# Grouped-query decode attention: K transposed on VectorE in 32x32 blocks of 4-byte words, scores and PV with K and V as the moving operand

## The chip, the cores and the metric

The kernel runs on one core of one Trainium2 chip. The metric is the device time of one execution in microseconds, as the median of a few executions. The profile's span (first to last instruction of the program) is about 1.8 us shorter than that time.

## The reference, cut to what matters

Two tokens (batch 2, one query each) attend to a long cache: 32 query heads share 8 K/V heads (`rep` = 4), 32,768 keys per head, head size 128, all bf16. A small MLP makes a gate.

```python
q = (x @ wq).reshape(B, Sq, Hq, Dh).transpose(0, 2, 1, 3)
scores = einsum("bhqd,bhkd->bhqk", q, repeat(k_cache, 4)) * Dh ** -0.5
o = einsum("bhqk,bhkd->bhqd", softmax(scores), repeat(v_cache, 4))
s = o.transpose(0, 2, 1, 3).reshape(B, 1, Hq * Dh) @ wo
...                                   # g = silu(MLP(layernorm(x)))
return x + s * g
```

K and V are 134 MB each, and every byte is used once. The weights are another 12 MB.

## The kernel before

The cache is cut into 32 pairs of a 4 MB K tile and a 4 MB V tile (16,384 keys each). One tile is 32 KB in each of the 128 partitions: 128 keys of 128 values. Tiles rotate through five slots, all loaded by the SyncE queue. `wo` is the last load, in three parts, into a slot that a K tile gives up.

```python
t = slot(name)                                     # 5 slots of [128, 16384] bf16
nc.sync.dma_start(out=t, in_=cache[b, g, i*NK:(i+1)*NK, :].rearrange("(p t) d -> p (t d)", p=128))
...
for n in range(NQ):                                # small loads of x, on ScalarE's queue
    nc.scalar.dma_start(out=x4_bf[32*n:32*n+B, :], in_=A_x[:, 0, n*QW:(n+1)*QW])
...
def emit_k(n):                                     # one K tile: 16 blocks of 8 x 128 keys
    for blk in range(NBLK):
        for j in range(TPB):                       # TensorE transposes K ...
            nc.tensor.transpose(out=tT[:, j, :], in_=kt[:, blk*TPB + j, :], identity=ident)
        # ... VectorE (3 of 4) or ScalarE (1 of 4) copies it out of PSUM ...
        nc.vector.tensor_copy(out=ktb, in_=tT)
        for j in range(TPB):                       # ... and K is the stationary operand
            nc.tensor.matmul(sc[:, u*rep:(u+1)*rep], lhsT=ktb[:, j, :], rhs=q4)
    nc.scalar.activation(out=ep, in_=sc, func=ACT.Exp, scale=inv_sqrt_dh)
...
def emit_v(n, ep):                                 # one V tile, V stationary
    for u in range(KPT):                           # 128 matmuls of 4 columns
        nc.tensor.matmul(o, lhsT=vt[:, u, :], rhs=ep[:, u*rep:(u+1)*rep], ...)
```

The softmax here doesn't subtract the row's maximum and nothing guards it: scores larger than these inputs give would overflow.

## Time and profile before

| | before |
|---|---|
| time, median of 3 runs | 682.95 us (682.73 to 683.0) |
| span of the profiled run | 681.2 us |
| busy: PE / DVE / ACT | 80% / 43% / 23% |
| DMA rate in the middle | 428 GB/s |

The first lines are from the page: the span, the busy time of each engine, the DMA engines' mean busy share and rate in 40 equal slices, two of the DMA queues (packets, MB, share of the 16 engines' time), and the chain of waits that ended last.

```profile
span 681.2 us, 26832 instructions
PE 548.0 (80%) x12728; PEld 533.1 (78%) x12728; DVE 294.5 (43%) x476; ACT 154.7 (23%) x168; POOL 1.1 (0%) x9
...
DMA  7999999999999999999999999999999999999965
GB/s 308 430 428 427 429 428 427 430 424 429 431 424 428 427 434 428 426 428 429 428 428 425 432 430 427 428 427 425 428 427 428 424 426 429 430 428 429 420 256 182
...
q1 hardware_dynamic: 13804, 280.50, 96.8%
q8 instruction: 99, 1.62, 1.0%
...
DMA 57%; PE 35%; issue 5%; ACT 2%; DVE 0%; ACTq 0%; POOL 0%; SPq 0%; DVEq 0%; POOLq 0%
```

From the second slice to the 38th the DMA engines are full: 280.5 MB at 428 GB/s are 655 of the 681 us. PE is busy, but it is not what the kernel waits for.

The view by stretches shows the start and the end closer. Its columns are the stretch and its length, busy time (and instructions) of PE, PEld, DVE, ACT and POOL, the granted TensorE clock, the mean busy share of the 16 DMA engines, and GB/s.

```profile
12.00:14.00 2.00, 0.04 (x1) 0.04 (x2) 1.92 (x6) 0.00 (x0) 0.00 (x0) 1.00 0.00 0
...
648.00:652.00 4.00, 4.00 (x82) 4.00 (x81) 2.51 (x4) 1.05 (x2) 0.00 (x0) 0.77 0.91 341
652.00:656.00 4.00, 4.00 (x102) 3.92 (x99) 2.84 (x5) 1.99 (x2) 0.00 (x0) 1.00 0.55 225
656.00:660.00 4.00, 3.11 (x94) 2.88 (x92) 1.90 (x3) 1.61 (x2) 0.00 (x0) 1.00 0.56 235
660.00:664.00 4.00, 2.79 (x89) 2.70 (x88) 0.35 (x2) 0.00 (x0) 0.00 (x0) 0.51 0.44 183
```

DMA moves nothing from 12 to 14 us: the queue of loads has been waiting for the load of `wq` to land, 11.8 us in all (total, times, longest):

```profile
SPq L75 <- DMA wq<-in_A_wq_dram: 11.8, 1, 11.8
```

From 652 us on it is half idle, although the last V tile and `wo` are still to come. The timeline of the end says when they came (start, duration, engine, line; in brackets the idle time before and what ended it):

```profile
665.92 3.57 PE L261 MATMUL o<-ep,v 128*128 128x4 bf16 x128 [3.13 <-DMA v<-in_A_v_cache_dram]
...
671.53 2.25 PE L305 MATMUL s_ps<-wo,oT_sb 128*2 128x128 bf16 x64 [2.04 <-DMA wo<-in_A_wo_dram]
...
675.77 1.97 PE L305 MATMUL s_ps<-wo,oT_sb 128*2 128x128 bf16 x64 [1.99 <-DMA wo<-in_A_wo_dram]
```

The last V tile (V31, requested at 623.1 us) landed at 665.9 us, parts of `wo` at 671.5 and 675.7.

### The profile page before, as it was taken

The page shows a single profiled execution, that of the slowest core. Times are in us where ns is not written, and L with a number is a line of the kernel's source. Part 1 is how long each engine was busy: PE and PEld are TensorE (multiplying, and loading weights), DVE is VectorE, ACT ScalarE, POOL GpSimd, SP SyncE. Part 2 cuts the span into 40 slices and gives each one's busy share as a digit, 9 for nine tenths or more (in the row PEclk, how much of TensorE's full clock was granted, in tenths as well). Part 3 has the DMA queues.
Part 4 walks back from the last instruction along what each step waited for, and adds up shares of the span by engine and source line. Part 5 has one row for each costly group of instructions (what it writes and reads, how often), then busy time and mean ns, then how long its engine had stood idle before and what let it go on. Part 6 is the DMA issues. An engine that isn't in the chain of part 4 may idle for free.

```text
span 681.2 us, 26832 instructions
## 1 busy us (share of the span) xinstructions
PE 548.0 (80%) x12728; PEld 533.1 (78%) x12728; DVE 294.5 (43%) x476; ACT 154.7 (23%) x168; POOL 1.1 (0%) x9
## 2 busy tenths in 40 slices
PE   0598798878879888878988878888887898887884
PEld 0587788878878888878887878888787888887783
DVE  2272454434455444435544344554344454443440
ACT  0042321212222121222211222221222222222220
POOL 0000000000000000000000000000000000000000
PEclk9995887667888766778876678987667887776785
DMA  7999999999999999999999999999999999999965
GB/s 308 430 428 427 429 428 427 430 424 429 431 424 428 427 434 428 426 428 429 428 428 425 432 430 427 428 427 425 428 427 428 424 426 429 430 428 429 420 256 182
DMA packets 13954, 282.22 MB, mean 414 GB/s; under 512 B 1162, under 2 KB 5268, under 8 KB 5268
## 3 DMA queue, kind: packets, MB, share of 16 engines
q1 hardware_dynamic: 13804, 280.50, 96.8%
q8 instruction: 99, 1.62, 1.0%
q14 instruction: 11, 0.09, 0.0%
q10 hardware_dynamic: 40, 0.01, 0.0%
HBM read 280.50 MB, written 0.00 MB: 412 GB/s over the span
## 4 chain that ended last, share of the span: by engine, by line
DMA 57%; PE 35%; issue 5%; ACT 2%; DVE 0%; ACTq 0%; POOL 0%; SPq 0%; DVEq 0%; POOLq 0%
DMA k<-in_A_k_cache_dram 48%; PE tT L230 21%; PE o L261 7%; PE sc L222 6%; DMA wo<-in_A_wo_dram 6%; ACT ktb L233 2%; DMA x_bf<-in_A_x_dram 1%; DMA xn_120<-xn 1%; PE S L270 0%; PE s_ps L305 0%; ACTq L87 0%; DVE stats_ln_127 L116 0%; DVE xn L123 0%; ACTq L134 0%; SPq L293 0%
## 5 line engine op out<-in xcount | busy, mean ns | idle before, releaser
L230 PE MATMUL tT<-ident,k 128*128 128x128 bf16 x3840 | 340.4, 245 | 29.5 <-DMA k<-in_A_k_cache_dram 23.6
L235 DVE COPY ktb<-tT 128x1024 bf16<-128x1024 bf16 x384 | 260.0, 692 | 167.6 <-PE tT L230 167.4
L230 PEld LDWEIGHTS <-k 128*128 128x128 bf16 x3840 | 269.7, 111 | 32.8 <-DMA k<-in_A_k_cache_dram 25.5
L233 ACT COPY ktb<-tT 128x1024 bf16<-128x1024 bf16 x128 | 129.5, 1012 | 474.2 <-PE tT L230 474.2
L222 PE MATMUL sc<-q_sb,ktb 128*128 128x4 bf16 x4096 | 180.6, 166 | 27.0 <-ACT ktb L233 21.2
L222 PEld LDWEIGHTS <-ktb 128*128 128x128 bf16 x4096 | 159.9, 99 | 35.2 <-ACT ktb L233 23.9
L261 PE MATMUL o<-ep,v 128*128 128x4 bf16 x3968 | 113.2, 166 | 42.4 <-issue 39.3
L261 PEld LDWEIGHTS <-v 128*128 128x128 bf16 x3968 | 108.7, 102 | 45.1 <-issue 41.9
L255 DVE TENSOR_REDUCE s<-ep 128x4 f32<-128x512 bf16 x32 | 22.0, 686 | 69.1 <-ACT ep L243 69.1
L275 DVE RECIPROCAL rec<-S 128x4 f32<-128x4 f32 x16 | 2.9, 183 | 59.9 <-PE S L270 59.9
L276 DVE TENSOR_TENSOR oT_sb<-o,rec 128x4 bf16<-128x4 f32 x16 | 2.6, 165 | 58.4 <-PE o L261 58.4
L243 ACT ACTIVATE ep<-sc 128x512 bf16<-128x512 f32 x32 | 19.1, 597 | 15.9 <-PE sc L222 15.9
L270 PE MATMUL S<-s,ones_f 128*128 128x4 f32 x64 | 18.0, 354 | 0.5 <-DVE t_f L204 0.5
L230 PE MATMUL tT<-ident,k_92 128*128 128x128 bf16 x128 | 11.5, 248 | 7.1 <-DMA k_92<-in_A_k_cache_dram 7.1
L270 PEld LDWEIGHTS S<-s,ones_f 128*128 128x128 f32 x64 | 16.0, 312 | 0.7 <-DVE t_f L204 0.7
L230 PEld LDWEIGHTS <-k_92 128*128 128x128 bf16 x128 | 9.1, 112 | 7.2 <-DMA k_92<-in_A_k_cache_dram 7.2
L146 PE MATMUL treg<-ident,xn_bf 2*128 2x2 bf16 x4 | 0.3, 171 | 14.0 <-DVE xn_bf L138 14.0
L146 PEld LDWEIGHTS <-xn_bf 2*128 2x128 bf16 x4 | 0.2, 113 | 14.0 <-DVE xn_bf L138 14.0
L230 PE MATMUL tT<-ident,k_94 128*128 128x128 bf16 x128 | 9.6, 218 | 0.8 <-issue 0.8
L305 PE MATMUL s_ps<-wo,oT_sb 128*2 128x128 bf16 x128 | 4.1, 306 | 4.1 <-DMA wo<-in_A_wo_dram 4.0
L230 PEld LDWEIGHTS <-k_94 128*128 128x128 bf16 x128 | 7.3, 97 | 0.0
L305 PEld LDWEIGHTS <-oT_sb 128*2 128x2 bf16 x128 | 3.1, 116 | 4.9 <-issue 2.7
(54 smaller groups left out, 40.6 us busy)
## 6 DMA issues: line engine op xcount, KB each, us to landing
v<-in_A_v_cache_dram SPq DMA_DIRECT2D x31, 4096.0 KB, 37.3
k<-in_A_k_cache_dram SPq DMA_DIRECT2D x30, 4096.0 KB
wq<-in_A_wq_dram SPq DMA_DIRECT2D x1, 4096.0 KB, 12.2
k_92<-in_A_k_cache_dram SPq DMA_DIRECT2D x1, 4096.0 KB, 13.5
k_94<-in_A_k_cache_dram SPq DMA_DIRECT2D x1, 4096.0 KB
v_99<-in_A_v_cache_dram SPq DMA_DIRECT2D x1, 4096.0 KB
w_96<-in_B_w_dram SPq DMA_DIRECT2D x2, 1792.0 KB
wo<-in_A_wo_dram SPq DMA_DIRECT2D x1, 2048.0 KB
```

Of the source, the lines that this page charges most:

```text
L146: nc.tensor.transpose(out=treg[:, c:c + B], in_=src[0:B, k::DK], identity=ident[0:B, 0:B])
L222: nc.tensor.matmul(sc[:, u * rep:(u + 1) * rep], lhsT=ktb[:, j, :], rhs=q4, start=True, stop=True,)
L230: nc.tensor.transpose(out=tT[:, j, :], in_=kt[:, blk * TPB + j, :], identity=ident[:, :])
L233: nc.scalar.copy(out=ktb[:, :, :], in_=tT[:, :, :])
L235: nc.vector.tensor_copy(out=ktb[:, :, :], in_=tT[:, :, :])
L243: nc.scalar.activation(out=ep[:, :], in_=sc[:, :], func=ACT.Exp, scale=inv_sqrt_dh)
L255: nc.vector.tensor_reduce(out=state["s"][:, i, :], in_=ep[:, :].rearrange("p (t h) -> p h t", h=rep), axis=AX.X, op=ALU.add,)
L261: nc.tensor.matmul(o[:, :], lhsT=vt[:, u, :], rhs=ep[:, u * rep:(u + 1) * rep], start=(i == 0 and u == 0), stop=(i == NPART - 1 and u == K ...
L270: nc.tensor.matmul(S[:, :], lhsT=ones_f[:, :], rhs=state["s"][:, j, :], start=(j == 0), stop=(j == NPART - 1),)
L275: nc.vector.reciprocal(out=rec[:, :], in_=S[:, :])
L276: nc.vector.tensor_mul(out=oT_sb[:, g * rep:(g + 1) * rep, b], in0=o[:, :], in1=rec[:, :],)
L305: nc.tensor.matmul(s_ps[32 * n:32 * n + B, :], lhsT=oT_sb[:, h, :], rhs=wo3[:, h, n * QW:(n + 1) * QW], start=(h == 0), stop=(h == Hq - 1) ...
```

## The change

The intent is to take work from TensorE. VectorE transposes K in 32x32 blocks of 4-byte words (two bf16 values at a time). A stationary operand `z` of 128 columns holds the queries block by block, zeros elsewhere, and K streams past it 512 columns at a time: 32 matmuls per tile instead of 128 transposes and 128 score matmuls. For PV, 16 columns of probabilities (4 keys x 4 heads) are stationary, four such tiles stand beside each other in the array, and V streams 512 columns at a time: 32 matmuls instead of 128. The eight small loads of x and its normalized copy also move from ScalarE's to GpSimd's queue.

```diff
-        nc.scalar.dma_start(out=x4_bf[32 * n:32 * n + B, :], in_=...)
+        nc.gpsimd.dma_start(out=x4_bf[32 * n:32 * n + B, :], in_=...)
 ... (the same for xn4)
-            for j in range(TPB):
-                nc.tensor.transpose(out=tT[:, j, :], in_=kt[:, blk * TPB + j, :], identity=ident[:, :])
-            nc.vector.tensor_copy(out=ktb[:, :, :], in_=tT[:, :, :])      # or nc.scalar.copy
-            ...  nc.tensor.matmul(sc[:, u * rep:(u + 1) * rep], lhsT=ktb[:, j, :], rhs=q4, ...)
+        for r in range(NR):                                   # 8 per tile
+            T = ktp.tile([128, W], I32, tag="T", name="T")    # W = 1024 words
+            nc.vector.transpose(out=T..., in_=kt[:, r * W:(r + 1) * W]...)
+            for nb in range(NB):
+                for e in range(2):
+                    nc.tensor.matmul(sc[:, :], lhsT=z[:, nb, e, zc:zc + 128], rhs=Tb[:, nb, :, e], ...)
-        nc.scalar.activation(out=ep[:, :], in_=sc[:, :], func=ACT.Exp, scale=inv_sqrt_dh)
+        nc.scalar.activation(..., accum_out=rs[:, :])
+        nc.vector.transpose(out=pt..., in_=ep...)             # probabilities, 512 elements
 ...
-        for u in range(KPT):
-            nc.tensor.matmul(o[:, :], lhsT=vt[:, u, :], rhs=ep[:, u * rep:(u + 1) * rep], ...)
+        for u in range(KPT // VT):
+            nc.tensor.matmul(
+                o[32 * j:32 * j + VT * rep, :],
+                lhsT=pt[:, r, a * VT * rep:(a + 1) * VT * rep],
+                rhs=vt[:, u * VT:(u + 1) * VT, :].rearrange("p t d -> p (t d)"),
+                tile_position=(0, 32 * j), ...)
 ... (per head group: a copy of o out of PSUM and 4 matmuls that sum and transpose it)
```

## The prediction

> **What bounds the kernel now.** The loads. In the table of 40 slices the DMA row is full from the second slice to about the 37th, at 424 to 434 GB/s, while PE is busy 80% of the span, DVE 43%, ACT 23%. K and V are 268 MB, weights 12 MB: 280.5 MB at 428 GB/s is 655 of the 681 us. One K+V pair (8.4 MB) needs 19.6 us; PE works about 17 us of each 20 (the table by stretches). The chain of waits is 57% DMA, "k" and at last "wo". So what PE saves in the middle is worth nothing; only the first 20 and last 35 us can change.
>
> **What the change does per pair** (estimates).
> - Removes 128 PE transposes, 128 score and 128 PV matmuls (about 17 us of PE) and their PSUM copies.
> - DVE: 8 transposes of 1024 words. The trace's 512-element reduction takes 686 ns, about one element per cycle plus 0.15 us; the Trainium skill (VectorE: DVE Perf Modes, "The three transpose paths") gives 311 ns for a 128x128 bf16 transpose, which fits; no run has yet shown it for 4-byte words. So about 1.2 us each, 9.8 us, plus 0.7 us for the probabilities: with waits about 13 us.
> - PE: 32 matmuls of 512 columns for scores and 32 column-tiled ones for PV. The skill (TensorE: Matmul & The Clock Gate, Part 1) gives 216 ns each warm, 427 cold: scores 7 to 14 us, PV 2 to 6 us. I expect 9 to 14.
>
> Both stay below 19.6 us, so steady state stays DMA-bound at 428 GB/s. K's slot is freed by DVE instead of PE, about as soon. From issue to landing a load takes 37 us: four loads outstanding on five slots, much slack.
>
> **Start.** The trace shows DMA moving nothing from 12 to 14.2 us: the queue waits ("wq" 11.8 us, "xn" 7.3 us) before issuing K0, K1, V0. By program order, the changed kernel issues wq, K0, K1, w3, w4, V0 without waits, because the eight small x loads moved to the GpSimd queue. The first 20 us moved 6.4 MB at 320 GB/s; 18 us at 428 would be 7.7 MB: about 3 us gained. Risk: the small loads land late behind 20 MB and delay q.
>
> **Tail.** V31 lands at 665.9 us, with DMA engines only half busy from 652 on; wo lands at 675.8. wo waits for K30's slot, as before. After V31: column-tiled PV (about 4 us cold), a PSUM copy and four fp32 matmuls (about 3 us more than now), close to wo's landing. So the tail gives back 0 to 2 us.
>
> **Prediction:** about 680 us, range 672 to 690. Faster by over 2%: 5%; within 2%: 81%; slower: 14%.
>
> **What would show it.** DMA row full and about 428 GB/s in the middle; the hole at 12 to 14 us gone; DVE transposes about 1.2 us each, DVE near 50 to 60%; score matmuls 0.22 to 0.43 us apart; PE below 65%; ACT near 5%; the chain of waits still mostly DMA k and wo.
>
> **What would make it wrong.** A 4-byte transpose at two cycles per element (2.3 us, over 18 us per pair) makes DVE the limit: about 700 us. Score matmuls slowed by the 4-byte step of the moving operand, or PV tiles not overlapping, on a cold clock: PE near 20 us per pair. A late q starving the queue near 48 us: some 5 us. Faster by 2% would need the half-idle DMA tail to disappear.

## More of the kernel before

Every `matmul` and `transpose` is two TensorE instructions, a weight load and a matmul, so a pair of tiles costs 768 of them. The compiled program has 25,369 TensorE instructions in all.

## The result, and the profile after

| | before | after |
|---|---|---|
| time, median of 4 runs | 682.89 us (682.73 to 683.0) | 666.06 us (665.98 to 666.11) |
| span | 681.2 us | 664.2 us |
| PE / DVE / ACT busy | 80% / 43% / 23% | 61% / 51% / 8% |

The ratio is 0.9754, with a 95% interval of 0.9737 to 0.977: faster by 2.5%. (A ratio is the mean time of one kernel's fast runs over that of the other's of the same rounds, so not quite the ratio of the medians.)

The same lines of the page of the changed kernel, then three of its groups of instructions (count, busy us, mean ns of one):

```profile
span 664.2 us, 6171 instructions
PE 403.1 (61%) x2588; PEld 172.5 (26%) x2620; DVE 340.1 (51%) x403; ACT 50.1 (8%) x152; POOL 7.4 (1%) x19
...
DMA  9999999999999999999999999999999999999996
GB/s 377 413 438 436 423 433 434 426 433 434 426 434 428 430 435 430 427 434 433 428 433 428 432 433 428 431 434 427 432 433 425 433 432 429 432 430 431 434 403 199
...
q1 hardware_dynamic: 13804, 280.50, 98.8%
q8 instruction: 20, 0.33, 0.2%
...
DMA 73%; PE 16%; DVE 7%; issue 3%; ACT 0%; POOL 0%; SPq 0%; DVEq 0%; ACTq 0%; POOLq 0%
...
L280 DVE STREAM_TRANSPOSE T<-k 128x1024 int32<-128x1024 int32 x240 | 273.9, 1207 | 173.7 <-DMA k<-in_A_k_cache_dram 173.7
L288 PE MATMUL sc<-T,z_123 128*128 128x512 bf16 x496 | 149.7, 463 | 97.0 <-DVE T L280 93.5
...
L320 PE MATMUL o<-v,pt 128*16 128x512 bf16 x992 | 67.0, 418 | 4.8 <-DMA v<-in_A_v_cache_dram 4.8
```

The stretches of the start and the end, and the end's timeline:

```profile
12.00:14.00 2.00, 0.00 (x0) 0.00 (x0) 0.00 (x0) 0.00 (x0) 0.00 (x0) 1.00 1.04 443
...
648.00:652.00 4.00, 3.59 (x32) 1.09 (x31) 0.00 (x0) 0.04 (x1) 0.00 (x0) 0.57 1.07 332
652.00:656.00 4.00, 2.12 (x72) 1.97 (x73) 0.17 (x1) 0.54 (x1) 0.00 (x0) 0.90 1.05 334
```

```profile
648.32 3.59 PE L320 MATMUL o<-v,pt 128*16 128x512 bf16 x32 [4.80 <-DMA v<-in_A_v_cache_dram]
...
658.54 2.01 PE L367 MATMUL s_ps<-wo,oT_sb 128*2 128x128 bf16 x64 [3.27 <-DMA wo<-in_A_wo_dram]
```

The hole at 12 to 14 us is gone, as predicted. The half-idle stretch at the end is gone too, which was not predicted: the rate there is 332 GB/s with the engines full (the 1 KB rows of `wo` move more slowly), not 225 with half of them idle. V31 lands at 648.3 instead of 665.9 us.

### Where the 17 us lie

A load is cut over 16 DMA engines, and each adds 1 to the load's semaphore when its sixteenth has landed. The Trainium skill says so (DMA: Bandwidth & Descriptors, "Why a DMA increments its semaphore by 16 and not by 1": only the full 16 means that all data landed), and the trace agrees: 16 increments are recorded for each K or V load. Sorted, they show how far the 16 engines have drifted apart. For V31, in us after the first of the 16 (worked out from the trace's semaphore records; the record does not say which engine an increment came from):

```
before, first at 645.4:  0 0.1 0.1 0.1 0.5 0.9 2.3 7.3 18.7 18.7 18.7 18.7 18.8 18.9 19.1 20.5
after,  first at 643.3:  0 0.1 0.2 0.2 0.4 0.7 0.8 3.2  3.3  3.3  3.4  3.6  4.1  4.7  5.0  5.0
```

I call the last number the spread. In both kernels the first sixteenths of successive loads land 9.7 us apart from the first tenth of the run to the last: the leading engines are never starved. What differs is the drift. Before, the spread was 6.4 us for a load landing at 205 us, 12.6 at 405 and 20.5 at 666, in eight laggards; after, it ends at 5.0. While tiles are in the queue, nobody sees the drift, because leaders work ahead on later loads. At the end there is nothing ahead, and the leaders idle: that is the half-busy DMA row.

The sum, in spans: the first sixteenth of V31 comes 2.1 us earlier, the spread is 15.5 us smaller, and from V31's landing to the end takes 0.6 us longer (15.9 against 15.3). 2.1 + 15.5 - 0.6 = 17.0 us, the whole difference.

What makes eight engines drift? Theory F: the fetching of TensorE's instructions. They are 64 bytes each (q8 moved 1.62 MB for 25,369 of them), which makes 99 blocks of 16 KB, and queue q8 shows 99 packets before and 20 after. The trace gives such a packet 1.06 us (mean), on the same DMA engines that carry K and V. 15.5 us over 79 blocks is 0.2 us of the end per block. Rival P: PE was pacing the kernel through the slots it frees (PE was 35% of the chain). Rival S: the start is worth more than its hole.

### The profile page after: what moved, and what is told of

It reads as the page before. It is cut to its first block, busy times and chain, and to the rows that moved or that the text cites. A ratio compares the mean times of both kernels' runs of the same rounds, so it can differ in the third digit from the quotient of the medians.

```text
span 664.2 us, 6171 instructions
## 1 busy us (share of the span) xinstructions
PE 403.1 (61%) x2588; PEld 172.5 (26%) x2620; DVE 340.1 (51%) x403; ACT 50.1 (8%) x152; POOL 7.4 (1%) x19
## 4 chain that ended last, share of the span: by engine, by line
DMA 73%; PE 16%; DVE 7%; issue 3%; ACT 0%; POOL 0%; SPq 0%; DVEq 0%; ACTq 0%; POOLq 0%
DMA k<-in_A_k_cache_dram 65%; PE sc L288 12%; DMA wo<-in_A_wo_dram 6%; DVE T L280 6%; PE o L320 3%; DMA x_bf<-in_A_x_dram 2%; DVE pt L299 1%; PE qT_ps L193 1%; ACT ep L297 0%; PE s_ps L367 0%; PE S L316 0%; POOL x_bf L95 0%; DVE stats_ln_146 L149 0%; DVE sm L315 0%; DVE ln_145 L156 0%
## 5 line engine op out<-in xcount | busy, mean ns | idle before, releaser
L280 DVE STREAM_TRANSPOSE T<-k 128x1024 int32<-128x1024 int32 x240 | 273.9, 1207 | 173.7 <-DMA k<-in_A_k_cache_dram 173.7
L288 PE MATMUL sc<-T,z_123 128*128 128x512 bf16 x496 | 149.7, 463 | 97.0 <-DVE T L280 93.5
L288 PE MATMUL sc<-T,z_124 128*128 128x512 bf16 x496 | 145.9, 453 | 95.9 <-DVE T L280 92.1
L288 PEld LDWEIGHTS <-z_123 128*128 128x128 bf16 x512 | 57.8, 113 | 187.1 <-issue 148.1
L288 PEld LDWEIGHTS <-z_124 128*128 128x128 bf16 x512 | 56.9, 111 | 184.8 <-issue 143.7
L320 PE MATMUL o<-v,pt 128*16 128x512 bf16 x992 | 67.0, 418 | 4.8 <-DMA v<-in_A_v_cache_dram 4.8
L299 DVE STREAM_TRANSPOSE pt<-ep 128x512 bf16<-128x512 bf16 x32 | 22.8, 712 | 79.6 <-ACT ep L297 79.6
L320 PEld LDWEIGHTS <-pt 128*16 128x16 bf16 x1024 | 24.8, 95 | 39.1 <-issue 20.2
L332 PE MATMUL oT<-sel_o,ob 128*128 128x4 f32 x128 | 16.9, 255 | 11.1 <-ACT ob L329 11.1
L332 PEld LDWEIGHTS oT<-sel_o,ob 128*128 128x128 f32 x128 | 15.5, 191 | 19.5 <-ACT ob L329 19.5
L311 DVE MEMSET o<- 128x512 f32 x16 | 7.8, 485 | 13.4 <-ACT ob L329 12.3
L280 DVE STREAM_TRANSPOSE T<-k_98 128x1024 int32<-128x1024 int32 x8 | 9.1, 1208 | 0.0
L280 DVE STREAM_TRANSPOSE T<-k_100 128x1024 int32<-128x1024 int32 x8 | 9.1, 1202 | 0.0
L264 ACT COPY z_123<-qr 32x16 bf16<-32x16 bf16 x32 | 6.3, 198 | 7.4 <-DVE qr L211 7.0
L264 ACT COPY z_124<-qr 32x16 bf16<-32x16 bf16 x32 | 6.3, 198 | 0.3
```

Source lines behind the costliest of these rows:

```text
L264: nc.scalar.copy(out=z[32 * j:32 * j + 32, :, :, c:c + rep], in_=qr[32 * j:32 * j + 32, :, :, b, g * rep:(g + 1) * rep],)
L280: nc.vector.transpose(out=T[:, :].rearrange("p (b t k) -> p t b k", b=NB, t=RT), in_=kt[:, r * W:(r + 1) * W].rearrange("p (t b k) -> p t ...
L288: nc.tensor.matmul(sc[:, :], lhsT=z[:, nb, e, zc:zc + 128], rhs=Tb[:, nb, :, e], start=(r == 0 and nb == 0 and e == 0), stop=(r == NR - 1 ...
L299: nc.vector.transpose(out=pt[:, :, :].rearrange("p r (t h) -> p t r h", h=rep), in_=ep[:, :].rearrange("p (t r h) -> p t r h", r=NR, h=rep),)
L311: nc.vector.memset(state["o"][:, :], 0.0)
L320: nc.tensor.matmul(o[32 * j:32 * j + VT * rep, :], lhsT=pt[:, r, a * VT * rep:(a + 1) * VT * rep], rhs=vt[:, u * VT:(u + 1) * VT, :].rearr ...
```

## The experiments

### The start alone (before_start)

The kernel before, with only the small loads moved:

```diff
-        nc.scalar.dma_start(out=x4_bf...        (and xn4)
+        nc.gpsimd.dma_start(out=x4_bf...
```

> The kernel before with one part of the change alone: the eight small x loads go to the GpSimd queue. Theory F (instruction fetch: 16 KB blocks of instructions are fetched by the same DMA engines as K and V, delay some of the 16 and so every load's last sixteenth; 99 blocks before, 20 after, about 0.2 us of the end per block): only the hole at 12 to 14 us goes, about 2 us faster (681), the last V load still lands about 20 us after its first sixteenth. Rival S (the start is the gain): about 668. Rival P (PE was pacing the slots): no change beyond the start.

Measured: 680.73 us against 682.93 (ratio 0.9967, 0.9952 to 0.9982). The hole is filled:

```profile
12.00:14.00 2.00, 0.00 (x0) 0.00 (x0) 0.00 (x0) 0.00 (x0) 0.00 (x0) 1.00 0.85 361
```

The trace shows what the queue had waited for: in the kernel before, K0's load signals the same semaphore as `wq`'s (number 102) and is issued at 13.4 us, once `wq` has landed; with the small loads on GpSimd's queue it has another one (113) and is issued at 1.6 us. The first sixteenth of V31 lands 2.5 us sooner (642.9) and the spread is unchanged at 20.4 us. The start is worth 2.2 us, and rival S falls.

### Half measures: fewer instructions by another road (before_pv, after_oldpv)

`before_pv` is the kernel before with the new PV alone; `after_oldpv` is the changed kernel with the old PV put back.

```diff
 before_pv
-        for u in range(KPT):
-            nc.tensor.matmul(o[:, :], lhsT=vt[:, u, :], rhs=ep[:, u * rep:(u + 1) * rep], ...)
+        for u in range(KPT // VT):
+            nc.tensor.matmul(o[32*j:32*j + 16, :], lhsT=ep[:, u*16:(u+1)*16],
+                             rhs=vt[:, u*4:(u+1)*4, :]..., tile_position=(0, 32*j), ...)
 after_oldpv: the reverse, with ptf[:, u * rep:(u + 1) * rep] as the moving operand
```

> The kernel before with the new PV alone: 32 column-tiled matmuls of 512 columns in place of 128. 19,290 PE instructions instead of 25,369, so 75 blocks instead of 99. Theory F: 24 blocks fewer at 0.2 us, about 4.7 us faster, near 678; spread of the last V load's landings 15 us instead of 20. Rival P: PE loses about 2 of 17 us per pair; some us faster too, but with the spread unchanged. Rival S: no change.

Measured: 680.44 us against 682.93 (0.9963, 0.9948 to 0.9978).

```profile
q8 instruction: 76, 1.25, 0.7%
```

The spread is 16.2 us, near the forecast, but the kernel is 2.5 us faster rather than 4.7. The first sixteenth of V31 came 1.1 us later than in the kernel before (646.5), and from V31's landing to the end took 15.9 us instead of 15.3; these two ate part of it. Some 0.3 us of the 1.1 was there by the first V tile; where the rest comes from was not tested.

> The changed kernel with the old PV (128 matmuls of 4 columns) put back: the new scores alone. 11,057 PE instructions, 43 blocks instead of 20. Theory F: 23 blocks more at 0.2 us, about 4.6 us slower than the changed kernel, near 671; spread about 9.5 us instead of 5. Rival P: PE has 1 to 2 us more per pair, far from a limit, so no change. Rival S: no change.

Measured: 670.78 us (0.9822 of before; 4.7 us more than the changed kernel's 666.06, which ran in another call).

```profile
q8 instruction: 43, 0.70, 0.4%
```

The spread is 9.8 us, the first sixteenth at 643.3 as in the changed kernel. As theory F said; neither rival expected a loss here.

### Work without instructions, instructions without work (after_busy, after_tiny)

These two part F from P. Both add dummy matmuls to the changed kernel after each V tile, with results that nobody reads. One adds 16 full matmuls per pair, the other 160 of one element:

```diff
 after_busy
+        for u in range(16):
+            nc.tensor.matmul(dum[:, :], lhsT=pt...[:, 0:128], rhs=vt[:, u*VT:(u+1)*VT, :]..., start=True, stop=True)
 after_tiny
+        for u in range(160):
+            nc.tensor.matmul(dum[0:1, u:u+1], lhsT=pt[:, 0, c:c+1], rhs=vt[:, 0, d:d+1], start=True, stop=True)
```

> The changed kernel with 16 more full 512-column matmuls per tile pair, results unused: 3.5 to 7 us more of PE per pair, so PE as busy as before, but only 1,024 more instructions (4 blocks). Theory F: about 0.8 us slower, near 667, spread about 6 us. Rival P (PE busy time paces the slots): most of the gain lost, 675 to 682.

> The changed kernel with 160 one-by-one matmuls per tile pair, results unused: 15,203 PE instructions, about 59 blocks of 16 KB instead of 20, little array work. Theory F: 39 blocks more at 0.2 us each, 7 to 8 us slower than the changed kernel, near 674, spread of the last V load about 13 us instead of 5. Rival P: the added issue time [...] with 11 us there comes near the 19.4 us pace: 666 to 680 with the spread unchanged at 5 us and the first sixteenths landing later.

Measured: `after_busy` 666.26 us (0.9757 of before, 0.9743 to 0.9772), `after_tiny` 676.32 us (0.9903, 0.9886 to 0.9919). Span, busy times and the instruction queue of each, `after_busy` first:

```profile
span 664.4 us, 7178 instructions
PE 507.6 (76%) x3083; PEld 216.9 (33%) x3132; DVE 340.1 (51%) x403; ACT 50.1 (8%) x152; POOL 7.4 (1%) x19
...
q8 instruction: 24, 0.39, 0.2%
```

```profile
span 674.5 us, 16411 instructions
PE 545.3 (81%) x7708; PEld 321.8 (48%) x7740; DVE 339.8 (50%) x403; ACT 50.2 (7%) x152; POOL 7.4 (1%) x19
...
q8 instruction: 60, 0.98, 0.6%
```

104 us more of PE busy time with 4 more blocks costs 0.2 us, and the spread stays at 5.1. 40 more blocks cost 10.3 us. In `after_tiny` the first sixteenth of V31 lands at 643.2 us, no later than in the changed kernel, so PE's load did not slow the queue; the spread is 12.6 us instead of 5.0, which is 7.6 of the 10.3 us. The rest is a side effect of the experiment: after V31 the dummy matmuls of the last tile stand in the chain that ends the kernel (the timeline has one run of 86 of them, 2.29 us, before the last head group's sums). `after_tiny` is not wholly without work: PE was busy 142 us longer than in the changed kernel, more than in `after_busy`. What clears rival P is `after_busy`, which has the work and keeps the gain, together with the first sixteenth that did not move here. Rival P falls.

### Instructions on an engine that does nothing else (after_pooldrain)

GpSimd is idle for nearly the whole run. Each pair gets 320 drain instructions on it, 10,240 in all:

```diff
+        for _ in range(320):
+            nc.gpsimd.drain()
```

> The changed kernel with 320 drain instructions per tile pair on GpSimd, which is idle: 10,240 more instructions, 40 blocks more, no work on PE, VectorE or data. Theory F: if its fetches meet the same DMA engines as PE's, 7 to 8 us slower (674); if others, less (they lag by themselves, 668 to 670). Rivals P and S: no change, 666.

Measured: 714.88 us (1.0468 of before, 1.0452 to 1.0483), far above what I expected. GpSimd's instructions are fetched by queue q14, whose line in the changed kernel was `q14 instruction: 6, 0.05, 0.0%`; here:

```profile
q14 instruction: 86, 0.70, 0.2%
q8 instruction: 20, 0.33, 0.2%
```

80 more blocks, of 8 KB this time. The sixteen landings of V31, after the first at 664.5 us:

```
after_pooldrain: 0 0.2 0.3 0.4 0.4 0.4 0.5 0.5 0.5 0.6 0.6 0.8 0.9 1.0 1.1 32.6
```

One engine lags 32.6 us behind fifteen that land within 1.1. All of GpSimd's blocks evidently go through one DMA engine (read from these landings). The spread passed 25 us before the middle of the run and stayed near 32: by then the leaders had used up every slot and had to wait, so the rate fell from 430 GB/s (100 to 300 us) to 400 (500 to 640 us). The end moved by 48.8 us, 0.6 us per block. This touches no engine that works on K or V, and it shows the mechanism at its plainest: a load is as late as its last sixteenth. My number was wrong because I had assumed a spread over several engines, as for TensorE.

### An attempt to beat both (after_wo8)

If eight engines lead at the end, the tail of `wo` could be given to them alone. I split its last quarter into transfers of 40, 40, 40 and 8 partitions.

```diff
-    wo_parts = [(0, 16), (16, 28), (28, 32)]
+    wo_parts = [(0, 16), (16, 24), (24, 32)]
+    # the last part: partitions 0:40, 40:80, 80:120, 120:128, one transfer each
```

> An attempt to beat both: the changed kernel with the last quarter of wo (1 MB) loaded by transfers of 40 and 8 partitions, which can be cut over 8 of the 16 DMA engines only. If those 8 are the ones that run ahead at the end by 3 to 5 us, moving 64 KB off each laggard (64 rows of 1 KB at 48 ns, 3 us) ends the loads up to 3 us sooner, 663 to 664; if they are the laggards, up to 3 us later, 669; if the transfers are spread over all 16 anyway, no change, 666.

Measured: 669.63 us, slower than the changed kernel by 3.6. The attempt rested on a mistake: a transfer of 40 partitions used 10 engines, not 8 (its semaphore shows 11 separate increments; one is the sequencer's for the unused rest). That is the rule of the skill (same page and section, "How many engines": the largest number up to 16 that divides the outer dimension), and I had applied it wrongly. Judging by the landings (the last transfer's run from 659.0 to 662.8 us), both the tens and the last eight included leaders and laggards, so that some laggards got more work; this was not tested. Which engines lag is not in the records; the changed kernel remains the best.

### All runs together

"Blocks" are the 16 KB packets of TensorE's instruction queue; V31 is the last V tile; times in us. (`after_pooldrain`, which adds another engine's blocks, and `after_wo8`, which changes the last load, are left out; they are given above.)

| run | blocks | V31 first | V31 last | spread | span | time |
|---|---|---|---|---|---|---|
| before | 99 | 645.4 | 665.9 | 20.5 | 681.2 | 682.9 |
| before_start | 99 | 642.9 | 663.3 | 20.4 | 678.9 | 680.7 |
| before_pv | 76 | 646.5 | 662.7 | 16.2 | 678.6 | 680.4 |
| after_tiny | 60 | 643.2 | 655.8 | 12.6 | 674.5 | 676.3 |
| after_oldpv | 43 | 643.3 | 653.1 | 9.8 | 669.0 | 670.8 |
| after_busy | 24 | 643.4 | 648.5 | 5.1 | 664.4 | 666.3 |
| after | 20 | 643.3 | 648.3 | 5.0 | 664.2 | 666.1 |

A line through `before` and `after` (0.196 us per block) gives 16.0, 12.8, 9.5 and 5.8 us for the four between them: within 0.7 us of each.

## Why the prediction was wrong, point by point

- **What bounds the kernel: right.** K and V at 428 GB/s set the pace before, and 431 after (100 to 640 us). Emptying PE in the middle was worth nothing, and `after_busy` shows that filling it again costs nothing.
- **VectorE's transposes: right.** 1207 ns were measured for 1.2 us. The estimate drawn from the skill's bf16 example (VectorE: DVE Perf Modes, "The three transpose paths": 311 ns for 128x128) carried over to 4-byte words: 1024 of them took 1207 ns where this trace's bf16 transpose of 512 elements took 712. VectorE's share was 51%, in the forecast 50 to 60%. (ScalarE's was 8%, where I had said near 5%.)
- **TensorE's cost: right.** Score matmuls came 225 ns apart where the granted clock was 1.00 (635 to 639 us) and 427 ns apart where it was 0.50 (631 to 634 us; spacing of the weight loads in the timeline). The skill gives 216 and 427 ns (TensorE: Matmul & The Clock Gate, "Wait — 56ns, not 53.3ns?"). 32 PV matmuls took 1.9 us at full clock, 59 ns each, so the tiles do overlap; 3.6 us at half clock.
- **The start: right, a little large.** 3 us predicted, 2.2 measured (`before_start`).
- **The tail: wrong, and this is the step that failed.** I wrote "V31 lands at 665.9 us, with DMA engines only half busy from 652 on" and "So the tail gives back 0 to 2 us". I took the half-idle tail for a property of the loads that the change leaves alone. It was the sum of a drift over the whole run, fed by TensorE's instruction blocks, and the change takes four fifths of those blocks away. V31 landed 17.6 us sooner, of which 15.5 are the drift.
- The prediction did name the sign: "Faster by 2% would need the half-idle DMA tail to disappear." It did disappear. I gave that 5%, because I never asked why some engines were slow. The page showed `q8 instruction` at 1.0% of the DMA engines' time; 1% of a DMA-bound 681 us is 6.8 us if shared equally over 16 engines, and about twice that if, as the landings suggest, eight carry it.

One thing the runs left open is answered by the packet records of their traces. 99 packets of 1.06 us over eight engines are 13 us for each, and the laggards were 19 to 20 us behind. The rest is lost on the packet that comes next. After the first 16 us of `before`, 104 of the 32 KB packets of K and V took over 1.4 us, where the median is 1.21. 94 of them begin within 0.02 us of the end of one of q8's packets and take 1.71 us on average, 0.50 more than the median; nine follow one of q14's, and one follows none. So a block costs its engine 1.06 + 0.50 = 1.56 us. Shared by eight engines that is 0.195 us per block, the 0.2 us of theory F: 19.4 us for 99 blocks and 3.9 for 20, where the laggards were measured at 18.7 to 20.5 and at 3.2 to 5.0. Why the packet behind a block is slow, the traces do not show.

The same records speak against a rival that no run was made for: that something else which grows with the number of instructions, such as the profiler's own notes of them, slows the loads. The 32 KB packets that took under 1.4 us are as quick before as after (1.216 and 1.217 us on average). That eight engines carry TensorE's blocks is read from the landings; the record names no engine, but the times of q8's packets repeat with a period of eight (1018, 1018, 1074, 1069, 1061, 1099, 1099, 1086 ns, and again). Before, packets eight apart differ by 8 ns on average, and those one to seven or nine apart by 26 or more.

## What to carry to other kernels

When loads set the pace, instructions are loads too: count them at 64 bytes, look at the queue lines of the page, and expect rewriting many small matmuls as a few large ones to pay even where PE was not the limit. A mean DMA share of one half while loads were outstanding meant here that some engines were done and others late; look at how far apart the sixteen landings of one load lie before you call the tail fixed. To test such a cause, add the suspected thing without its work (empty instructions) and the work without the thing (a few large matmuls).

## What the Trainium skill lacked or had wrong

- Runtime: NRT & Kernel Launch, "Instruction fetch mechanics": it says that each sequencer drives its own DMA queue for instructions and refills them in 16 KiB blocks, which the trace confirms for TensorE (99 packets of 16,384 bytes for 25,369 instructions of 64 bytes). It also says that crossing a block is "mostly hidden". In this DMA-bound kernel it was not: each block of TensorE's moved the end by about 0.2 us, 15.5 us for the 79 blocks that the change took away.
- The same section gives 16 KiB for every engine; GpSimd's blocks were 8 KB here (80 packets for 10,240 instructions).
- No page that I found says over which DMA engines the blocks go. TensorE's delayed eight of the sixteen sixteenths (18.7 to 20.5 us), GpSimd's a single one (32.6 us, while the others stayed within 1.1), which made 80 small blocks cost 48.8 us.
- VectorE: DVE Perf Modes, "The three transpose paths": this section has no time for 4-byte words; 128 x 1024 of them took 1207 ns.
